# Cluster attention with two MLPs: similarities of heads 0 and 1 by float32 products, centroid words split later

## The chip, the core and the metric

The program runs on one core of one Trainium2 chip. The time is device microseconds (us) from start to end of one execution. Five engines work beside each other, each through its own list of instructions in order: TensorE (PE, products), VectorE (DVE), ScalarE (ACT), GpSimd (POOL) and SyncE (SP, which issues transfers). They wait for each other by semaphores.

## What is computed

```python
q_n, k_n, c_n = (x / (norm(x) + 1e-6) for x in (q, k, centroids))
q_assign = argmax(einsum('bhsd,hcd->bhsc', q_n, c_n))      # 16 clusters per head
k_assign = argmax(einsum('bhsd,hcd->bhsc', k_n, c_n))
mask = q_assign[:, :, :, None] == k_assign[:, :, None, :]
scores = where(mask, q @ k.T / 8, -1e9)
attn = exp(scores - max(scores)); attn /= sum(attn) + 1e-9
x = attn @ v                                               # 2 x 8 heads, 768 x 64
x = gelu-like MLP (512 -> 2048 -> 512), then gated MLP (512 -> 1536 -> 512)
```

q, k, v are 2 x 8 x 768 x 64, the centroids 8 x 16 x 64; all is float32.

## The kernel before

The 16 heads run one after the other; the two MLPs follow, planned by a list scheduler that the change leaves alone. All of the change lies in the first part, before and in the first two heads, whose order on each engine is the order in which the code is written.

A head's q and k come as one tile `stage` (q in partitions 0 to 63, k in 64 to 127, 768 columns). TensorE multiplies in float32r, so each of q and k is split in a high word (a cast, by `hi_q`, `hi_k` or single copies) and a low word (what is left, a subtraction by `lo_q`, `lo_k`). The tiles `q2`, `k2` hold these words in part 0; part 1 holds the high words and, in rows 64 to 79, the one-hot rows of the clusters. `extra_rows` clears part 1 of a head's tiles by three memsets on GpSimd.

The assignment of a head goes through these steps. `similar` multiplies the words of q and k by the centroids' words `cs`: four products of 128 x 384 into one PSUM tile `sims`. `largest` transposes that on VectorE (`T`, in 32 x 32 blocks), adds the two parts that belong to high and low words of the centroids (L603), and takes the maximum and a weighting; `assign` finishes the one-hot and transposes it back (`oT`, two halves). The q rows of the one-hot are then written by ScalarE (L637), the k rows by GpSimd (L638, two casts of 16 x 384). After that `smax` multiplies part 1 of q2 by part 1 of k2 and VectorE reduces the result to row maxima (`nm`); `mrow` and `st` follow, and the exponentials `p` on ScalarE.

For `cs` the centroids are normalised on VectorE (`cn`, L538), transposed by TensorE into the PSUM tile `ctp` (L543), split into `ch` and `cl` on VectorE (L552, L553) and spread by three ScalarE copies (L557, L559). `keep_warm(n)` is n products of zeros that nobody reads. `load_qk(h)` are two transfers by SyncE, which wait until `stage` is free. Four `stage` tiles and five slots of `q2`, `k2` go round.

The one-hot of head 0 is made in a stretch of its own; that of head 1 beside the scores of head 0, and `smax` of head 1 is TensorE's next work after the last scores of head 0.

Of the kernel before, what the change touches and what calls it, by code (L numbers as in the profile page):

```python
# [8 lines left out]
F32 = mybir.dt.float32  # L9
# [3 lines left out]
ACTF = mybir.ActivationFunctionType  # L13
ALU = mybir.AluOpType
# [170 lines left out]
def tile_cluster_attention_two_mlps(ctx: ExitStack, tc: tile.TileContext, qk, v, cen, w1, w2, wg, wv, w3, out):  # L185
# [233 lines left out]
    def q2(h):  # L419
        return q2_t[h % NQK]  # L420

    def k2(h):
        return k2_t[h % NQK]

    def load_qk(h):
        b, hh = divmod(h, H)
        for i in range(2):
            nc.sync.dma_start(out=stage[h % NST][i * D:(i + 1) * D], in_=qk[b, hh, :, i, :])
# [9 lines left out]
    def hi_q(h, copy=nc.scalar.copy):  # L438
        src = stage[h % NST][0:D].unsqueeze(1)
        copy(q2(h)[0:D], src.to_broadcast([D, 2, S]))  # L440

    def hi_k(h):
        src = stage[h % NST][D:2 * D]
        nc.scalar.copy(k2(h)[D:2 * D, 0, :], src)
        nc.scalar.copy(k2(h)[0:D, 1, :], src)

    def lo_q(h, eng=nc.vector):
        t = q2(h)
        eng.tensor_tensor(
            out=t[D:2 * D, 0, :], in0=stage[h % NST][0:D], in1=t[0:D, 0, :].bitcast(F32), op=ALU.subtract  # L450
        )

    def lo_k(h, eng=nc.vector):
        t = k2(h)
        eng.tensor_tensor(
            out=t[0:D, 0, :], in0=stage[h % NST][D:2 * D], in1=t[D:2 * D, 0, :].bitcast(F32), op=ALU.subtract
        )
# [32 lines left out]
    def keep_warm(n):  # L490

        ps = ps_o.tile([128, 512], F32, tag="o", name="warm")
        for _ in range(n):
            nc.tensor.matmul(out=ps, lhsT=zeros[:, 0:128], rhs=zeros)  # L494
# [7 lines left out]


    LEAD = 128 - 2 * NC
    nc.gpsimd.memset(cs.bitcast(F32), 0.0)

    def extra_rows(i):
        for t in (q2_t[i], k2_t[i]):
            nc.gpsimd.memset(t[D:MROW, 1, :].bitcast(F32), 0.0)
        nc.gpsimd.memset(k2_t[i][MROW:MROW + 1, 1, :].bitcast(F32), 1.0)  # L510
# [3 lines left out]
    for i in range(NC):  # L514
        nc.vector.memset(wd[:, :, i:i + 1], float(NC - i))
    nc.gpsimd.memset(v_t[0][:, :, D:D + 1], 1.0)
    for i in range(1, 3):
        extra_rows(i)
    s1 = acst.tile([128, 1], F32, name="s1")
    s2 = acst.tile([128, 1], F32, name="s2")  # L520
    for i in range(4):
        nc.gpsimd.memset(s1[32 * i:32 * i + 32], 1.0 if i % 2 else BIG)
        nc.gpsimd.memset(s2[32 * i:32 * i + 32], -1.0 if i % 2 else 0.0)


    sq = am_p.tile([128, HALF], F32, tag="U", name="U")[:, 0:D]
    nc.vector.tensor_tensor(out=sq, in0=craw, in1=craw, op=ALU.mult)
# [13 lines left out]
    ctp = ps_x.tile([128, 128], F32, tag="x", name="ctp")  # L541
    keep_warm(7)
    nc.tensor.transpose(out=ctp, in_=cn.rearrange("p a d -> p (a d)"), identity=ident)  # L543
    keep_warm(5)


    ks, qs = stage[0][D:2 * D], stage[0][0:D]
    nc.scalar.copy(q2(0)[0:D, 0, :], qs)
    nc.scalar.copy(k2(0)[D:2 * D, 0, :], ks)
    ch = acst.tile([128, 128], F32R, name="ch")  # L550
    cl = acst.tile([128, 128], F32R, name="cl")
    nc.vector.tensor_copy(ch, ctp)  # L552
    nc.vector.tensor_tensor(out=cl, in0=ctp, in1=ch.bitcast(F32), op=ALU.subtract)  # L553
    lo_q(0)
    to = cs[:, :, LEAD:].rearrange("p i (h x) -> p i h x", x=128)
    of = [t.rearrange("p (h c) -> p h c", c=NC) for t in (ch, cl)]
    nc.scalar.copy(to[:, :, :, 0:NC], of[0].unsqueeze(1).to_broadcast([128, 2, H, NC]))  # L557
    for i, r in enumerate((slice(0, D), slice(D, 2 * D))):
        nc.scalar.copy(to[r, i, :, NC:2 * NC], of[1][r])  # L559
    lo_k(0)  # L560
    nc.scalar.copy(k2(0)[0:D, 1, :], ks)
    nc.scalar.copy(q2(0)[0:D, 1, :], qs)
    ident_r = acst.tile([128, 128], F32R, name="ident_r")

    def similar(hs, pl=ps_x, tag="x"):


        out = []
        for h in hs:
            ps = take_bank(pl, tag, [128, 512], "sims")[:, 0:HALF]  # L570
            todo = [(i, n) for i in (0, 1) for n in range(2)]
            for at, (i, n) in enumerate(todo):
                o = LEAD + 128 * (h % H) - 32 * (2 * n + i)
                nc.tensor.matmul(  # L574
                    out=ps,
                    lhsT=cs[:, i, o:o + 128],
                    rhs=(q2, k2)[i](h)[:, 0, n * HALF:(n + 1) * HALF],
                    start=(at == 0),
                    stop=(at == len(todo) - 1),
                )  # L580
            out.append(ps)
        return out
# [9 lines left out]
    def largest(hs, pss):  # L592


        T = T_t[hs[0]] = am_p.tile([128, HALF], F32, tag="T", name="T")
        for j, ps in enumerate(pss):
            U = T if len(hs) == 1 else am_p.tile([128, HALF], F32, tag="U", name="U")
            nc.vector.transpose(out=U, in_=ps)
            yield
            of = U.rearrange("p (g a c) -> p g a c", a=2, c=NC)  # L600
            to = T.rearrange("p (g a c) -> p g a c", a=2, c=NC)[:, :, j, :]
            if len(hs) == 1:
                nc.vector.tensor_tensor(out=to, in0=of[:, :, 0, :], in1=of[:, :, 1, :], op=ALU.add)  # L603
            else:
                nc.vector.tensor_reduce(out=to.unsqueeze(3), in_=of.rearrange("p g a c -> p g c a"), axis=AX.X, op=ALU.add)
            yield
        Tv = groups(hs, T)
        G = Tv.shape[1]
        mx = sm_p.tile([128, HALF // NC, 1], F32, tag="mx", name="mx")[:, 0:G]
        nc.vector.tensor_reduce(out=mx, in_=Tv, axis=AX.X, op=ALU.max)  # L610
        yield
        nc.vector.tensor_tensor(out=Tv, in0=Tv, in1=mx.to_broadcast([128, G, NC]), op=ALU.is_equal)
        yield
        nc.vector.tensor_tensor(out=Tv, in0=Tv, in1=wd.to_broadcast([128, G, NC]), op=ALU.mult)  # L614
        yield
# [3 lines left out]
    def assign(hs, copies=(nc.scalar.copy, nc.scalar.copy)):  # L619

        T = T_next[0] = T_t.pop(hs[0])
        Tv = groups(hs, T)
        G = Tv.shape[1]
        mx2 = sm_p.tile([128, HALF // NC, 1], F32, tag="mx", name="mx2")[:, 0:G]
        nc.vector.tensor_reduce(out=mx2, in_=Tv, axis=AX.X, op=ALU.max)
        yield
        nc.vector.tensor_tensor(out=Tv, in0=Tv, in1=mx2.to_broadcast([128, G, NC]), op=ALU.is_equal)
        yield
        if len(hs) == 2:
            nc.vector.tensor_scalar(out=Tv, in0=Tv, scalar1=s1, scalar2=s2, op0=ALU.mult, op1=ALU.add)  # L630
        yield
        oT = am_p.tile([64, 2, HALF], F32, tag="oT", name="oT")
        for n in range(2):
            nc.vector.transpose(out=oT[:, n, :], in_=T[64 * n:64 * n + 64, :])  # L634
            if len(hs) == 1:
                rows = slice(ONE, ONE + NC), 1, slice(n * HALF, (n + 1) * HALF)
                nc.scalar.activation(q2(hs[0])[rows], oT[0:NC, n, :], ACTF.Copy, scale=BIG, bias=-BIG)  # L637
                nc.gpsimd.tensor_copy(k2(hs[0])[rows], oT[32:32 + NC, n, :])  # L638
            yield
        for j, h in enumerate(hs if len(hs) == 2 else ()):  # L640
            for i, dst in enumerate((q2(h), k2(h))):
                to = dst[ONE:ONE + NC, 1, :]
                o = 32 * i + NC * j
                rows = oT[o:o + NC].rearrange("p n s -> p (n s)")
                if j == 0:
                    copies[i](to, rows)
                else:
                    nc.sync.dma_start(out=to.bitcast(F32), in_=rows)

    def do(steps):  # L650
        for _ in steps:
            pass
# [213 lines left out]
    takes = {}  # L866
    for h in range(5, 5 + EARLY_ITEMS, 2):
        takes.update({(h, 2): (0,), (h, 3): (1,), (h, 4): (0,), (h, 5): (2,), (h + 1, 3): (1, 2)})
    sims = similar([0])
    keep_warm(18)  # L870
    hi_k(1)
    dummy = sm_p.tile([128, 1], F32, tag="dummy", name="dummy")
    nc.scalar.activation(dummy, y0, ACTF.Exp)
    do(largest([0], sims))

    do(assign([0]))
    hi_q(1)
    nc.vector.tensor_copy(ident_r, ident)
    lo_k(1, nc.gpsimd)
    lo_q(1, nc.gpsimd)  # L880
    hi_k(2)
    lo_k(2, nc.gpsimd)
    extra_rows(3)
    load_qk(4)
    load_qk(5)
    maxima = [(c, n) for m in range(2) for c in range(3 * m, 3 * m + 3) for n in range(2)]
    for i in range(SC):
        smax(0, *maxima[i], *((ps_m, "m"), (ps_m, "m"), (ps_s, "s"), (ps_s, "s"), (ps_s, "s"))[i % 5])
# [9 lines left out]
    for c in range(SC):  # L898
        scores(0, c, 0)
        if c < 2:  # L900
            smax(0, *maxima[10 + c], ps_m, "m")
        if c == 1:
            mneg(0, slice(SC // 2, SC))
            sims = similar([1])
            do(largest([1], sims))
        if c == 3:
            mrow_at_once(0, 1, ps_o, "o")
    for c in range(SC):
# [801 lines left out]
```

## Time and profile before

| | us |
|---|---|
| median of 3 runs | 769.22 (769.13 to 771.26) |
| the profiled execution | 769.23 |
| its span, first to last instruction | 767.4 |
| PE busy in the span | 759.5 |
| DVE busy | 667.4 |
| ACT busy | 492.9 |
| POOL busy | 148.6 |

The span is shorter than the time by 1.83 us, which lie before the first and behind the last instruction. TensorE is the engine that is nearly always busy; a change at the program's head is worth what it moves the start of TensorE's unbroken work.

### The profile page before, as it was taken

How to read it: one execution, taken by the hardware profiler on the slowest of the kernel's cores; microseconds unless marked ns; L12 is line 12 of the kernel's file. 1: busy time of each engine (PE TensorE's matmuls, PEld its weight loads, DVE VectorE, ACT ScalarE, POOL GpSimd, SP SyncE). 2: the span in 40 equal slices, each digit the busy share in tenths (PEclk: the TensorE clock that was granted, in tenths of full speed). 3: DMA queues.
4: the chain of work that ended last, by engine and by line, in shares of the span. 5: the costliest groups of instructions: out<-in, count | busy, mean ns of one | idle time of the engine just before them, and what ended most of it. 6: DMA issues, size and time to landing. Idle time of an engine off the chain costs nothing.

```text
span 767.4 us, 11983 instructions
## 1 busy us (share of the span) xinstructions
PE 759.5 (99%) x4194; PEld 659.5 (86%) x4194; DVE 667.4 (87%) x1224; ACT 492.9 (64%) x861; POOL 148.6 (19%) x165
## 2 busy tenths in 40 slices
PE   8999999999999999999999999999999999999998
PEld 6996676767677999999999999999999999999996
DVE  7899899999966999999797889999987997877752
ACT  7867798886686887677676776676453644443322
POOL 8847465746452000000000000000000000000000
PEclk9999999999999999999999999999999999999999
DMA  4132365843215787633277763667232122312102
GB/s 122 45 103 70 94 164 126 212 100 71 75 42 186 259 257 228 196 132 111 95 259 243 266 221 124 222 215 241 94 124 94 56 83 96 128 53 83 56 0 83
DMA packets 53388, 104.11 MB, mean 136 GB/s; under 512 B 19776, under 2 KB 25264, under 8 KB 53328
## 3 DMA queue, kind: packets, MB, share of 16 engines
q1 hardware_dynamic: 53104, 103.02, 43.1%
q8 instruction: 33, 0.54, 0.3%
q10 hardware_dynamic: 224, 0.33, 0.2%
q14 instruction: 27, 0.22, 0.1%
HBM read 76.23 MB, written 21.06 MB: 127 GB/s over the span
## 4 chain that ended last, share of the span: by engine, by line
PE 88%; DVE 10%; issue 1%; ACT 1%; DVEq 0%; ACTq 0%
PE h L384 37%; PE a L384 29%; PE st L711 7%; PE pv L749 6%; PE smax L661 4%; DVE nm L666 3%; PE ps L749 2%; PE pv L820 1%; PE sims L574 1%; DVE b L379 1%; PE warm L494 0%; DVE wo L291 0%; DVE T L614 0%; DVE s L1253 0%; DVE oT L634 0%
## 5 line engine op out<-in xcount | busy, mean ns | idle before, releaser
L384 PE MATMUL h<-xc,b 128*128 128x384 f32 x1680 | 316.6, 337 | 0.1
L384 PEld LDWEIGHTS h<-xc,b 128*128 128x128 f32 x1680 | 291.6, 188 | 10.0 <-DVE u L1309 2.3
L384 PE MATMUL a<-g,sp 128*128 128x512 f32 (+1 forms) x768 | 144.3, 336 | 0.0
L384 PEld LDWEIGHTS a<-g,sp 128*128 128x128 f32 x768 | 124.9, 188 | 16.9
L384 PE MATMUL a<-sp,g 128*128 128x512 f32 x432 | 109.6, 393 | 0.0
L721 ACT ACTIVATE p<-st 128x384 f32<-128x384 f32 x192 | 88.0, 491 | 28.4 <-PE st L711 23.4
L666 DVE TENSOR_REDUCE nm<-smax 128x1 f32<-128x384 f32 x192 | 97.1, 554 | 5.9 <-PE smax L661 5.4
L711 PE MATMUL st<-q,k 128*128 128x384 f32 (+1 forms) x384 | 98.3, 346 | 0.1
L384 PEld LDWEIGHTS a<-sp,g 128*128 128x128 f32 x432 | 80.1, 188 | 13.2
L376 ACT CAST b<-s 128x512 fp32r<-128x512 f32 x80 | 49.5, 620 | 55.5 <-PE h L384 45.7
L711 PEld LDWEIGHTS st<-q,k 128*128 128x128 f32 (+1 forms) x384 | 68.2, 190 | 10.4 <-issue 7.8
L737 POOL TENSOR_TENSOR add<-add,p 128x384 f32<-128x384 f32 x78 | 76.2, 1007 | 0.0
L661 PE MATMUL smax<-k,q 80*128 80x384 f32 x192 | 63.6, 347 | 1.4 <-DVE nm L666 0.6
L1309 DVE TENSOR_TENSOR u<-h,p 128x384 f32<-128x384 f32 x80 | 44.3, 554 | 22.8 <-PE h L384 22.6
L749 PE MATMUL pv<-p,v 128*64 128x384 f32 x336 | 60.2, 494 | 0.0
L280 ACT ACTIVATE a<-raw 128x512 f32<-128x512 f32 x68 | 45.7, 672 | 19.0 <-issue 9.4
L379 DVE TENSOR_TENSOR b<-s,b 128x512 fp32r<-128x512 f32 x80 | 54.8, 687 | 1.9 <-ACT b L376 0.7
L379 DVE TENSOR_TENSOR g<-c,g 128x768 fp32r<-128x768 f32 x56 | 53.5, 969 | 1.5 <-ACT g L376 0.9
L376 ACT CAST g<-c 128x768 fp32r<-128x768 f32 x56 | 45.3, 835 | 12.4 <-DVE c L1324 11.8
L286 DVE SCALAR_TENSOR_TENSOR t<-a,t 128x512 int32<-128x512 int32 x68 | 46.1, 684 | 3.4 <-ACT t L283 3.4
L1317 ACT ACTIVATE c<-c 128x384 f32<-128x384 f32 (+1 forms) x56 | 38.3, 685 | 16.5 <-DVE c L1309 15.8
L376 ACT CAST b<-w 128x768 fp32r<-128x768 f32 x35 | 29.2, 835 | 29.7 <-PE h L384 29.6
(146 smaller groups left out, 913.5 us busy)
## 6 DMA issues: line engine op xcount, KB each, us to landing
raw<-in_w SPq DMA_DIRECT2D x44, 512.0 KB
w<-scr SPq DMA_DIRECT2D x30, 512.0 KB
raw<-in_wg SPq DMA_DIRECT2D x12, 512.0 KB
raw<-in_wv SPq DMA_DIRECT2D x12, 512.0 KB
w<-scrg SPq DMA_DIRECT2D x12, 512.0 KB
w<-scrv SPq DMA_DIRECT2D x12, 512.0 KB
st<-in_qk SPq DMA_DIRECT2D x31, 192.0 KB
scr<-wd SPq DMA_DIRECT2D x23, 256.0 KB
```

Of the source, the lines that this page charges most:

```text
L280: nc.scalar.activation(a, raw[:, :, 1].bitcast(F32), ACTF.Copy, scale=2.0**-112)
L286: nc.vector.scalar_tensor_tensor(out=t, in0=a.bitcast(I32), scalar=3, in1=t, op0=ALU.logical_shift_left, op1=ALU.bitwise_or)
L376: nc.scalar.copy(to, of)
L379: eng.tensor_tensor(out=to, in0=of, in1=hi.bitcast(F32), op=ALU.subtract)
L384: nc.tensor.matmul(out=out_ps, lhsT=lhs[a], rhs=rhs[b], start=(start and j == 0), stop=(stop and j == 2), skip_group_check=True, **kw)
L661: nc.tensor.matmul(out=ps, lhsT=q2(h)[0:ONE + NC, 1, c * 128:(c + 1) * 128], rhs=k2(h)[0:ONE + NC, 1, n * HALF:(n + 1) * HALF],)
L666: nc.vector.tensor_reduce(out=nm_t[h][:, c, n:n + 1], in_=ps, axis=AX.X, op=ALU.max)
L711: nc.tensor.matmul(out=ps, lhsT=k2(h)[0:rows, a, c * 128:(c + 1) * 128], rhs=q2(h)[0:rows, a, at], start=(a == 0), stop=(a == 1),)
L721: nc.scalar.activation(p_t[h, c][:, n * HALF:(n + 1) * HALF], ps, ACTF.Exp, scale=scale)
L737: nc.gpsimd.tensor_tensor(out=add_t[h][:, at], in0=before[:, at], in1=p_t[h, c][:, at], op=ALU.add)
L749: nc.tensor.matmul(out=ps[n * D:(n + 1) * D, 0:HALF], lhsT=w, rhs=x[:, n * HALF:(n + 1) * HALF], start=start, stop=stop, skip_group_check= ...
L1309: lambda: nc.vector.tensor_tensor(out=to.tile[:, part], in0=ps.tile[:, 0:HALF], in1=other.tile, op=ALU.add),
```

## The change

Heads 0 and 1 get their similarities from `similar_first`: two float32 products (no split into words) of the whole `stage` tile, one for each half of the 768 columns, with the weights `first_w`, 128 x 64 for a head: the centroids stand in columns 0 to 15 for the q partitions and in columns 32 to 47 for the k partitions, zeros elsewhere. The halves land in partitions 0 to 63 and 64 to 127 of the same PSUM tile. `first_w` is cleared on GpSimd and filled by two small VectorE copies from `ctp`. In `largest` the addition for one head falls away.

Around it, work is moved. The high word of q of head 0 is cast on VectorE, its k low word is made on GpSimd after the one-hot's casts, `ch` is cast on ScalarE from `ctp` and `cl` subtracted on GpSimd; the three copies into `cs` stand behind `hi_q(1)`. The identity's cast goes to ScalarE. One `keep_warm` has 2 products in place of 5. The activation that brings the table of exponentials stands ahead of ScalarE's casts. Of head 2, the second copy of k's high word becomes a transfer (`bits`), and `extra_rows(2)` and the memsets of `s1`, `s2` stand behind `lo_k(2)` on GpSimd. `load_qk(5)` is issued after the similarities of head 1.

```diff
     nc.gpsimd.memset(v_t[0][:, :, D:D + 1], 1.0)
-    for i in range(1, 3):
-        extra_rows(i)
+    extra_rows(1)
...
-    keep_warm(5)
+    keep_warm(2)
+    nc.scalar.activation(dummy, y0, ACTF.Exp)
     ks, qs = stage[0][D:2 * D], stage[0][0:D]
-    nc.scalar.copy(q2(0)[0:D, 0, :], qs)
+    nc.vector.tensor_copy(q2(0)[0:D, 0, :], qs)
+    for i, rows in enumerate((slice(0, D), slice(D, 2 * D))):
+        nc.vector.tensor_copy(
+            first_w[rows, :, 2 * NC * i:2 * NC * i + NC], ctp[rows, 0:2 * NC].rearrange("p (h c) -> p h c", c=NC)
+        )
+    def similar_first(h, pl, tag):
+        ps = take_bank(pl, tag, [128, 512], "sims")[:, 0:HALF]
+        for n in range(2):
+            nc.tensor.matmul(
+                out=ps[n * D:(n + 1) * D], lhsT=first_w[:, h], rhs=stage[h][:, n * HALF:(n + 1) * HALF],
+                start=True, stop=True, skip_group_check=True,
+            )
+        return [ps]
+    sims = similar_first(0, ps_s, "s")
+    keep_warm(18)
+    lo_q(0)
...
-    nc.vector.tensor_copy(ch, ctp)
-    nc.vector.tensor_tensor(out=cl, in0=ctp, in1=ch.bitcast(F32), op=ALU.subtract)
+    nc.scalar.copy(ctf, ctp)
+    nc.scalar.copy(ch, ctp)
+    nc.scalar.copy(ident_r, ident)
+    nc.gpsimd.tensor_tensor(out=cl, in0=ctf, in1=ch.bitcast(F32), op=ALU.subtract)
...
-            if len(hs) == 1:
-                nc.vector.tensor_tensor(out=to, in0=of[:, :, 0, :], in1=of[:, :, 1, :], op=ALU.add)
...
     do(assign([0]))
+    lo_k(0, nc.gpsimd)
     hi_q(1)
-    nc.vector.tensor_copy(ident_r, ident)
     lo_k(1, nc.gpsimd)
     lo_q(1, nc.gpsimd)
-    hi_k(2)
+    centroid_words()
+    nc.scalar.copy(k2(2)[D:2 * D, 0, :], stage[2][D:2 * D])
+    bits(k2(2)[0:D, 1, :], k2(2)[D:2 * D, 0, :])
     lo_k(2, nc.gpsimd)
+    extra_rows(2)
     extra_rows(3)
+    for i in range(4):
+        nc.gpsimd.memset(s1[32 * i:32 * i + 32], 1.0 if i % 2 else BIG)
+        nc.gpsimd.memset(s2[32 * i:32 * i + 32], -1.0 if i % 2 else 0.0)
     load_qk(4)
-    load_qk(5)
...
-            sims = similar([1])
-            do(largest([1], sims))
+            do(largest([1], similar_first(1, ps_x, "x")))
+            load_qk(5)
```

VectorE, from the centroids' normalised tile `cn` to the one-hot of head 0 (`q_0` and `k_0` are the word tiles of head 0, `st` a `stage` tile), before:

```order
L538 TENSOR_SCALAR cn<-craw,y_262 128x128
L552 CAST ch<-ctp 128x128
L553 TENSOR_TENSOR cl<-ctp,ch 128x128
L449 TENSOR_TENSOR q_0_165<-st_194,q_0_165 64x768
L455 TENSOR_TENSOR k_0_166<-st_194,k_0_166 64x768
L598 STREAM_TRANSPOSE T<-sims 128x384
L603 TENSOR_TENSOR T<-T 128x12x16
L610 TENSOR_REDUCE mx<-T 128x12
```

The same place now:

```order
L535 TENSOR_SCALAR cn<-craw,y_253 128x128
L546 CAST q_0_165<-st_194 64x768
L548 COPY first_w<-ctp 64x2x16 x2
L449 TENSOR_TENSOR q_0_165<-st_194,q_0_165 64x768
L618 STREAM_TRANSPOSE T<-sims 128x384
L628 TENSOR_REDUCE mx<-T 128x12
```

The split of the centroids and the low word of k have left VectorE's list, a cast and two copies have come, and the addition is gone.

GpSimd, from the one-hot casts of head 0 (`k_0<-oT`) to those of head 1 (`k_1<-oT`), before:

```order
L638 CAST k_0_166<-oT 16x384 x2
L455 TENSOR_TENSOR k_1_189<-st_195,k_1_189 64x768
L449 TENSOR_TENSOR q_1_188<-st_195,q_1_188 64x768
L455 TENSOR_TENSOR k_2_181<-st_196,k_2_181 64x768
L509 MEMSET q_3_175 32x768
L509 MEMSET k_3_176 32x768
L510 MEMSET k_3_176 1x768
L638 CAST k_1_189<-oT 16x384 x2
```

The same place now (eight memsets of 32 x 1 stand between the last two rows):

```order
L656 CAST k_0_166<-oT 16x384 x2
L455 TENSOR_TENSOR k_0_166<-st_194,k_0_166 64x768
L455 TENSOR_TENSOR k_1_189<-st_195,k_1_189 64x768
L449 TENSOR_TENSOR q_1_188<-st_195,q_1_188 64x768
L455 TENSOR_TENSOR k_2_181<-st_196,k_2_181 64x768
L511 MEMSET q_2_180 32x768
L511 MEMSET k_2_181 32x768
L512 MEMSET k_2_181 1x768
L511 MEMSET q_3_175 32x768
L511 MEMSET k_3_176 32x768
L512 MEMSET k_3_176 1x768
...
L656 CAST k_1_189<-oT 16x384 x2
```

A subtraction, three large memsets and eight small ones have come between the two pairs of casts.

## Rows read from the trace of the kernel before

**Rows 1.** The page: busy time of engines, and POOL in 40 slices.
```profile
PE 759.5 (99%) x4194; PEld 659.5 (86%) x4194; DVE 667.4 (87%) x1224; ACT 492.9 (64%) x861; POOL 148.6 (19%) x165
...
POOL 8847465746452000000000000000000000000000
```

**Rows 2.** Chain that ended last, in time: start us, us, what, up to `smax`.
```profile
4.91 0.46 PE ctp L543
...
7.02 0.96 DVE k L455
...
8.12 0.60 PE sims L574 x2
...
8.75 0.59 DVE T L598
...
9.37 0.37 DVE T L603
...
11.71 0.58 DVE oT L634
...
13.05 0.43 PE smax L661
```

**Rows 3.** Timeline of PE, several windows: start us, us, engine, line, instructions, idle before.
```profile
1.52 3.36 PE L494 MATMUL warm<-q 128*128 128x512 f32 x7 [1.52 <-DVE y L498]
...
6.01 0.88 PE L494 MATMUL warm<-q 128*128 128x512 f32 x3
...
25.83 0.74 PE L661 MATMUL smax<-k,q 80*128 80x384 f32 x3
...
59.95 1.51 PE L749 MATMUL pv<-p,v 128*64 128x384 f32 x8
...
61.79 2.80 PE L749 MATMUL pv<-p,v 128*64 128x384 f32 x16
```

**Rows 4.** Timeline of DVE, the head of the program and two later places.
```profile
4.35 0.41 DVE L538 TENSOR_SCALAR cn<-craw,y 128x128 f32<-128x128 f32 x1
5.39 0.29 DVE L552 CAST ch<-ctp 128x128 fp32r<-128x128 f32 x1 [0.63 <-PE ctp L543]
...
24.40 0.95 DVE L440 CAST q<-st 64x1536 fp32r<-64x1536 f32 x1
...
36.31 2.07 DVE L614 TENSOR_TENSOR T<-T,wd 128x384 f32<-128x384 f32 x1
...
41.41 0.55 DVE L646 CAST q<-oT 16x768 fp32r<-16x768 f32 x1
```

**Rows 5.** Timeline of ACT up to the one-hot rows of head 0.
```profile
3.27 0.20 ACT L531 ACTIVATE y<-ss 128x1 f32<-128x1 f32 x1 [0.46 <-DVE ss L530]
...
8.45 0.83 ACT L444 CAST k<-st 64x768 fp32r<-64x768 f32 x1
...
10.15 1.28 ACT L873 ACT_TABLE_LOAD   x1
...
12.38 1.07 ACT L637 ACTIVATE q<-oT 16x384 fp32r<-16x384 f32 x2 [0.73 <-DVE oT L634]
```

**Rows 6.** Timeline of POOL, memsets, one-hot casts and subtractions.
```profile
5.68 0.73 POOL L509 MEMSET q<- 32x768 f32 x1
...
10.11 0.09 POOL L522 MEMSET s<- 32x1 f32 x1
...
12.35 1.16 POOL L638 CAST k<-oT 16x384 fp32r<-16x384 f32 x2 [1.61 <-DVE oT L634]
13.59 1.83 POOL L455 TENSOR_TENSOR k<-st,k 64x768 fp32r<-64x768 f32 x1
...
19.25 0.73 POOL L509 MEMSET q<- 32x768 f32 x1
...
24.43 1.29 POOL L638 CAST k<-oT 16x384 fp32r<-16x384 f32 x1
...
35.94 2.04 POOL L449 TENSOR_TENSOR q<-st,q 64x768 fp32r<-64x768 f32 x1
```

More of the change, by code (lines that the diff above doesn't have):

```diff
@@ L504, in tile_cluster_attention_two_mlps @@
     LEAD = 128 - 2 * NC
+    first_w = acst.tile([128, 2, D], F32, name="first_w")
+    nc.gpsimd.memset(first_w, 0.0)
     nc.gpsimd.memset(cs.bitcast(F32), 0.0)
@@ L516, in tile_cluster_attention_two_mlps @@
     nc.gpsimd.memset(v_t[0][:, :, D:D + 1], 1.0)
-    for i in range(1, 3):
-        extra_rows(i)
+    extra_rows(1)
     s1 = acst.tile([128, 1], F32, name="s1")
     s2 = acst.tile([128, 1], F32, name="s2")
-    for i in range(4):
-        nc.gpsimd.memset(s1[32 * i:32 * i + 32], 1.0 if i % 2 else BIG)
-        nc.gpsimd.memset(s2[32 * i:32 * i + 32], -1.0 if i % 2 else 0.0)
     sq = am_p.tile([128, HALF], F32, tag="U", name="U")[:, 0:D]
@@ L543, in tile_cluster_attention_two_mlps @@
     nc.tensor.transpose(out=ctp, in_=cn.rearrange("p a d -> p (a d)"), identity=ident)
-    keep_warm(5)
+    keep_warm(2)
+    dummy = sm_p.tile([128, 1], F32, tag="dummy", name="dummy")
+    nc.scalar.activation(dummy, y0, ACTF.Exp)
     ks, qs = stage[0][D:2 * D], stage[0][0:D]
-    nc.scalar.copy(q2(0)[0:D, 0, :], qs)
+    nc.vector.tensor_copy(q2(0)[0:D, 0, :], qs)
[3 more added lines that the diff above has]
+        )
@@ L549, in tile_cluster_attention_two_mlps @@
+    def similar_first(h, pl, tag):
[9 more added lines that the diff above has]
+    lo_q(0)
     nc.scalar.copy(k2(0)[D:2 * D, 0, :], ks)
+    nc.scalar.copy(k2(0)[0:D, 1, :], ks)
@@ L550, in tile_cluster_attention_two_mlps @@
+    nc.scalar.copy(q2(0)[0:D, 1, :], qs)
+    ctf = acst.tile([128, 128], F32, name="ctf")
     ch = acst.tile([128, 128], F32R, name="ch")
     cl = acst.tile([128, 128], F32R, name="cl")
-    nc.vector.tensor_copy(ch, ctp)
-    nc.vector.tensor_tensor(out=cl, in0=ctp, in1=ch.bitcast(F32), op=ALU.subtract)
[L554 to L562, printed above, removed]
-    ident_r = acst.tile([128, 128], F32R, name="ident_r")
+    nc.scalar.copy(ctf, ctp)
+    nc.scalar.copy(ch, ctp)
+    ident_r = acst.tile([128, 128], F32R, name="ident_r")
+    nc.scalar.copy(ident_r, ident)
+    nc.gpsimd.tensor_tensor(out=cl, in0=ctf, in1=ch.bitcast(F32), op=ALU.subtract)
@@ L565, in similar, with centroid_words @@
+    def centroid_words():
+        to = cs[:, :, LEAD:].rearrange("p i (h x) -> p i h x", x=128)
+        of = [t.rearrange("p (h c) -> p h c", c=NC) for t in (ch, cl)]
+        nc.scalar.copy(to[:, :, :, 0:NC], of[0].unsqueeze(1).to_broadcast([128, 2, H, NC]))
+        for i, r in enumerate((slice(0, D), slice(D, 2 * D))):
+            nc.scalar.copy(to[r, i, :, NC:2 * NC], of[1][r])
     def similar(hs, pl=ps_x, tag="x"):
@@ L599, in largest @@
             yield
-            of = U.rearrange("p (g a c) -> p g a c", a=2, c=NC)
-            to = T.rearrange("p (g a c) -> p g a c", a=2, c=NC)[:, :, j, :]
-            if len(hs) == 1:
-                nc.vector.tensor_tensor(out=to, in0=of[:, :, 0, :], in1=of[:, :, 1, :], op=ALU.add)
-            else:
+            if len(hs) == 2:
+                of = U.rearrange("p (g a c) -> p g a c", a=2, c=NC)
+                to = T.rearrange("p (g a c) -> p g a c", a=2, c=NC)[:, :, j, :]
                 nc.vector.tensor_reduce(out=to.unsqueeze(3), in_=of.rearrange("p g a c -> p g c a"), axis=AX.X, op=ALU.add)
@@ L868, in tile_cluster_attention_two_mlps @@
         takes.update({(h, 2): (0,), (h, 3): (1,), (h, 4): (0,), (h, 5): (2,), (h + 1, 3): (1, 2)})
-    sims = similar([0])
-    keep_warm(18)
     hi_k(1)
-    dummy = sm_p.tile([128, 1], F32, tag="dummy", name="dummy")
-    nc.scalar.activation(dummy, y0, ACTF.Exp)
     do(largest([0], sims))
     do(assign([0]))
+    lo_k(0, nc.gpsimd)
     hi_q(1)
-    nc.vector.tensor_copy(ident_r, ident)
     lo_k(1, nc.gpsimd)
     lo_q(1, nc.gpsimd)
-    hi_k(2)
+    centroid_words()
+    nc.scalar.copy(k2(2)[D:2 * D, 0, :], stage[2][D:2 * D])
+    bits(k2(2)[0:D, 1, :], k2(2)[D:2 * D, 0, :])
     lo_k(2, nc.gpsimd)
+    extra_rows(2)
     extra_rows(3)
+    for i in range(4):
+        nc.gpsimd.memset(s1[32 * i:32 * i + 32], 1.0 if i % 2 else BIG)
+        nc.gpsimd.memset(s2[32 * i:32 * i + 32], -1.0 if i % 2 else 0.0)
     load_qk(4)
-    load_qk(5)
     maxima = [(c, n) for m in range(2) for c in range(3 * m, 3 * m + 3) for n in range(2)]
```

## Prediction, made before the changed kernel ran

> **What bounds the kernel now.** I read the page first: TensorE is busy for 759.5 of 767.4 us [rows 1], so 7.9 us is all that it waits, and an edit at the head of the program pays only if TensorE's unbroken work begins earlier. GpSimd's slices show where a second engine counts: it is busy in the first third and idle behind it. The chain of waits, in order of time, then says what the head consists of [rows 2]: the transposed centroids at 4.91, the splits on VectorE up to the low word of k (7.02 to 7.98), the last two similarity products at 8.12, VectorE's one-hot from 8.75 to the transposes at 11.71, the first maxima's product at 13.05. Last I read the timelines of single engines [rows 3 to 6], to see who is next when this chain gets shorter. The next place is the first products `smax` of head 1: the second of them starts at 25.83 [rows 3], 0.11 us after GpSimd's second one-hot cast of head 1 ends (24.43 + 1.29 = 25.72, [rows 6]). In the kernel before, GpSimd and TensorE arrive there together.
>
> **Step 1, the similarities of head 0.** VectorE is done with `cn` at 4.76 [rows 4]. The new cast of q is 768 columns wide; the row of that width took 0.55 [rows 4], so it runs from 4.79 to 5.34, behind the transpose, whose result VectorE took up at 5.39 [rows 4]. The two copies into `first_w` read 32 columns each from PSUM; the row with 128 columns took 0.29, so each lies between nothing and 0.29; I take 0.2, nearer to that row since its fixed part is in it. They end at 5.82, and with the 0.14 from VectorE to TensorE that rows 2 show (7.98 to 8.12) the products could start at 5.96. TensorE has two zero products to do first; the third of the old five started at 6.01 [rows 3], so that is the start. Their price is that of `pv`, which has the same shape (64 weights wide, 384 columns, float32, both halves): eight records in 1.51 and sixteen in 2.80, that is 0.16 a record and 0.22 behind the last [rows 3]. Two products are four records, so 0.87, and they end at 6.88. This is at the full clock of 2.4 GHz: the seven zero products from 1.52 took 0.48 each, near 512 columns at 1.2 GHz (0.43), the three from 6.01 took 0.29 each with their tail, near 2.4 GHz, and TensorE had worked without a break from 1.52 on. If the two products fall at the lower level they take 1.73 by the same rows. VectorE's transpose starts at 6.92 in place of 8.75: 1.83 earlier. `lo_q(0)` ends by 6.8 and hides under the products. The addition falls away (0.37 and its gap, 0.39, [rows 2]). Together **2.22 earlier** at the one-hot transposes.
>
> **Step 2, a collision on the way.** `cl` is now subtracted on GpSimd when `ch` is there, at about 8.2, while VectorE is in `is_equal` and the weighting, two operations with two inputs in SBUF. Rows show such a pair excluding each other: VectorE's weighting at 36.31 took 2.07, to 38.38, against GpSimd's subtraction from 35.94 to 37.98 [rows 4, 6], though half the width costs 0.37 [rows 2]. A subtraction of 768 columns takes 1.83 [rows 6], so one of 128 lies between 0.3 and 0.5. I charge 0.25; bounds 0 and 0.5. That leaves **1.97**. ScalarE is no gate: from 3.47, a table load of 1.28, 0.2 for its activation, five casts at 0.85 and three small ones at 0.3 end at 10.14, and the one-hot's first half comes at 12.38 less 1.97 = 10.41 [rows 5]. The 18 zero products, too, end before `smax`, at about 11.
>
> **Step 3, GpSimd between two heads.** Its casts for head 0 start at 12.35 less 1.97 = 10.38. Then, before those of head 1: the two casts with their gap 1.24 (12.35 to 13.59); four subtractions, one more than before, at 1.89 (three of them from 13.59 to 19.25); two `extra_rows`, one more than before, at 2.21 (two of them from 5.68 to 10.11); eight memsets of 0.09, at most 0.7 [rows 6]. Sum 1.24 + 7.55 + 4.43 + 0.7 = 13.92, so head 1's casts can start at 24.30. The one-hot of head 1 is there much earlier, its addition being gone as well: GpSimd is the gate. Undisturbed the casts take 1.16 and end at 25.46.
>
> **Step 4, what delays GpSimd more.** In the old trace its second cast took 1.29 in place of 0.58, since VectorE's cast of head 2's q ran from 24.40 to 25.35 [rows 4, 6]: while that cast holds, GpSimd stands, a loss of 0.71. Now VectorE reaches that cast at about 22, when GpSimd is in its memsets. No row has such a memset against such a cast: the cost is between nothing and 0.95, the cast's length. The nearest row, the cast on GpSimd, gives 0.71, and I take that, since a memset writes SBUF as the cast did. The casts of head 1 then start at 25.01 and end at 26.17, and the second `smax` starts at 26.28, against 25.83: **0.45 later than before**.
>
> The Trainium skill's page "SBUF — State Buffer", section "Who interferes with whom", says that a VectorE cast in its two-port mode and a GpSimd operation exclude each other for a whole instruction, and that only operations with two SBUF inputs spare a GpSimd operation that merely writes. By that rule the memsets stand behind the cast and the sum is 769.7; if merely writing spared them here too, it would be 769.0. The trace agrees for a cast on GpSimd (1.29 against 0.58); for a memset no run here shows it.
>
> **What follows.** TensorE's list has `smax` of head 1 next, so it waits for GpSimd whatever it gained: its own arrival would be 25.83 less 1.97 = 23.86. Behind that place TensorE, VectorE and GpSimd go on with the same lists as before, and the shift goes through to the end. GpSimd and VectorE keep their distance to about 0.1, so the collision at 36.31 stays. Costed at nothing: the `cs` copies (ScalarE has from 12.9 to 15, before the row of maxima is due), the transfer that replaces a copy of head 2 (needed some 25 us later; behind it on SyncE wait only loads of head 4 and later, used after 25), `load_qk(5)`, which had to wait for GpSimd's low words of head 1 anyhow, and the two float32 products of head 1 (0.65 by the records, four products of 0.16 before).
>
> The profiled execution took 769.23, the median is 769.22, so the sum stands against both: 769.23 + 0.45 = **769.7**.
>
> **Rivals.**
> - *Memsets are not held up by a cast.* Then GpSimd ends at 25.46, the second `smax` starts at 25.57: 0.26 gained, **769.0**. For it: no memset row is visibly stretched. Against it: the stretched cast. Without the collision of step 2 it is 768.7.
> - *GpSimd is no gate*, because its rows are rough and the memsets overlap more than I add. Then TensorE's own 1.97 come through: **767.3**. Against it: 1.7 to 2.4 us would have to vanish from a sum of 13.9.
> - *The similarity products fall at the lower clock*, or VectorE's first cast has to stand behind a memset (0.6 late, a like price): 0.87 more through the chain to GpSimd, **770.6**. Against it: the clock rose at about 6.0 while TensorE worked without a break, as it does now.
> - *Slower: TensorE loses its clock while it waits for GpSimd.* It would wait from 23.86 to 26.28, 2.4 us, and rows show no such hole. If the granted clock then falls to 1.2 GHz and comes back as slowly as at the start (at the lower level from 1.52 to about 6.0, [rows 3]), 4.5 us of work take twice their time: 2.25 more, **771.9**. It decides from the wait's length on: the 0.63 to 1.61 us for which engines wait in these rows are shorter, and none of them is TensorE's.
> - *The change doesn't do what it says*, the two float32 halves running one by one at some higher price than `pv`: that goes with the 770.6.
>
> The skill's "TensorE: Matmul & The Clock Gate", section "What's actually happening", says that the throttled clock is the default and activity releases it, which bears on the slower rival; whether this wait is long enough no run here shows.
>
> **How the numbers follow.** Chances: forecast 0.44; memsets not held up 0.32; GpSimd no gate 0.05; lower clock or a late cast 0.08; TensorE's clock lost 0.08; the rest, delays further on that I don't see, 0.03. About 0.3% (2.3 us, so below 766.9 or above 771.5) can be told from no change by a measurement of this kernel. The range reaches from 768.4 (the second case without the collision and with copies that cost nothing) to 770.9 (the lower clock, with the cast's full 0.95): it holds the first two and the fourth case, 0.84. Faster by over 0.3% takes the third case and more, 0.03; slower is the clock's loss and part of the rest, 0.09; within is 0.88.
>
> **What would show it.** The two float32 products near 6.0 and together about 0.9 long; the transposes of head 0's one-hot at 9.5 to 9.8; GpSimd's casts of head 1 at 25.0 (24.3 in the rival), with no idle time before them; a memset of about 1.5 us beside VectorE's cast at 22; TensorE waiting about 2 us ahead of `smax` of head 1. The forecast is wrong if GpSimd idles there, or if the time moves by over 1 us behind 26 us.

## The result and the profile after

The changed kernel takes 775.58 us (median of 22 runs, 768.85 to 777.45), the kernel before 769.64 (22 runs, 768.90 to 771.26): a ratio of 1.0056, with a 95% interval of 1.0039 to 1.0073. It is slower, by 5.9 us; the forecast was 769.7, a tie.

The runs of the changed kernel fall in two groups, told apart by TensorE's mean granted clock, and these groups are the finding. In 15 runs the clock was 0.988 to 0.991 and the time 775.47 to 777.45 (median 776.35); in 7 runs it was 0.999 or 1.000 and the time 768.85 to 770.47 (median 769.59, level with before). No run of the kernel before is below 0.999 (55 runs beside the experiments). The profiled execution is of the first group: 777.21, with a span of 775.4.

The page of the changed kernel: busy times, which answer to [rows 1], and the granted clock in 40 slices.

```profile
PE 767.2 (99%) x4191; PEld 665.6 (86%) x4191; DVE 664.5 (86%) x1221; ACT 491.4 (63%) x862; POOL 151.2 (19%) x168
...
PEclk9689999999999999999999999999999999999999
```

TensorE is busy 7.7 us longer with three instructions fewer, and the second and third slices (19 to 58 us) show a 6 and an 8 where the clock was granted in part. Both are seen closer in TensorE's timeline (start, us, engine, line, instructions, idle time before and who ended it):

```profile
6.11 0.87 PE L556 MATMUL sims<-st,first_w 128*64 128x384 f32 x4
...
22.73 1.31 PE L729 MATMUL st<-q,k 128*128 128x384 f32 x6
25.21 1.46 PE L679 MATMUL smax<-k,q 80*128 80x384 f32 x4 [1.17 <-POOL k L656]
26.47 2.65 PE L838 MATMUL pv<-v,p 128*128 128x65 f32 x12
...
39.91 2.12 PE L729 MATMUL st<-q,k 128*128 128x384 f32 x6
41.83 2.07 PE L838 MATMUL pv<-v,p 128*128 128x65 f32 x12
43.70 1.30 PE L729 MATMUL st<-q,k 128*128 128x384 f32 x6
44.84 1.45 PE L838 MATMUL pv<-v,p 128*128 128x65 f32 x12
...
49.83 0.95 PE L679 MATMUL smax<-k,q 80*128 80x384 f32 x4
```

The similarities stand at 6.11 and last 0.87. At 24.04 TensorE has reached `smax` of head 1 and waits 1.17 for GpSimd. Behind that, twelve `pv` products take 2.65 (26.47) where the same twelve take 1.45 at 44.84; six `st` products take 2.12 (39.91) and then 1.30 (43.70). Stretches of this trace (window, its us, PE busy and instructions, granted clock, DMA share, GB/s) say why:

```profile
25.50:26.00 0.50, 0.49 (x3) 1.00 0.00 0
26.00:26.50 0.50, 0.50 (x4) 0.55 0.00 0
...
42.50:43.00 0.50, 0.50 (x4) 0.50 0.00 0
43.00:44.00 1.00, 1.00 (x9) 0.94 0.00 0
```

1.00 is 2.4 GHz and 0.50 is 1.2 GHz, and a stretch with a value in between holds some time at each. 0.55 from 26.00 to 26.50 is 0.05 us at the upper level and 0.45 at the lower: the clock falls at about 26.05, 0.8 us behind the end of the wait. 0.94 from 43.00 to 44.00 puts its rise at about 43.12. In between, for 17.1 us, TensorE works at the lower level without a pause. `smax` of head 2 starts at 49.83; the kernel before has it at 42.67, 7.16 earlier. The rows of the kernel before at this place, with the first `smax` of head 1 and the `pv` behind it:

```profile
25.65 0.92 PE L661 MATMUL smax<-k,q 80*128 80x384 f32 x4
26.41 1.45 PE L820 MATMUL pv<-v,p 128*128 128x65 f32 x12
...
42.67 0.93 PE L661 MATMUL smax<-k,q 80*128 80x384 f32 x4 [0.43 <-DVE k L646]
```

GpSimd's and VectorE's timelines show what TensorE waited for, first GpSimd:

```profile
10.28 1.04 POOL L656 CAST k<-oT 16x384 fp32r<-16x384 f32 x2 [1.20 <-DVE oT L652]
...
22.52 0.73 POOL L512 MEMSET k<- 1x768 f32 x1
23.29 0.81 POOL L902 MEMSET s<- 32x1 f32 x1
...
24.51 0.09 POOL L903 MEMSET s<- 32x1 f32 x1
24.66 0.95 POOL L656 CAST k<-oT 16x384 fp32r<-16x384 f32 x2
```

```profile
7.01 0.58 DVE L618 STREAM_TRANSPOSE T<-sims 128x384 f32<-128x384 f32 x1
...
9.58 1.18 DVE L652 STREAM_TRANSPOSE oT<-T 64x384 f32<-64x384 f32 x2
...
22.46 1.60 DVE L440 CAST q<-st 64x1536 fp32r<-64x1536 f32 x1
```

A memset of 32 x 1 takes 0.81 beside VectorE's cast of head 2's q, against 0.09 for the others; the cast itself, 0.95 in the kernel before [rows 4], takes 1.60. The memset of 22.52 runs at its usual 0.73 to 23.25, so it is the cast that stood behind it first, and the next two memsets behind the cast.

### The profile page after: what moved, and what is told of

Same layout as the page of the kernel before. It is cut to its first block, busy times and chain, and to the rows that moved or that the text cites. A ratio compares the mean times of both kernels' runs of the same rounds, so it can differ in the third digit from the quotient of the medians.

```text
span 775.4 us, 11982 instructions
## 1 busy us (share of the span) xinstructions
PE 767.2 (99%) x4191; PEld 665.6 (86%) x4191; DVE 664.5 (86%) x1221; ACT 491.4 (63%) x862; POOL 151.2 (19%) x168
## 4 chain that ended last, share of the span: by engine, by line
PE 87%; DVE 7%; POOL 1%; DMA 1%; ACT 1%; issue 1%; SPq 0%; POOLq 0%; ACTq 0%; DVEq 0%
PE h L384 38%; PE a L384 30%; PE st L729 6%; PE pv L767 5%; DVE nm L684 3%; PE smax L679 3%; PE pv L838 2%; PE ps L767 2%; PE sims L594 1%; DMA st<-in_qk 1%; POOL k L455 0%; DVE oT L652 0%; DVE st L472 0%; DVE wo L291 0%; DVE t L286 0%
## 5 line engine op out<-in xcount | busy, mean ns | idle before, releaser
L679 PE MATMUL smax<-k,q 80*128 80x384 f32 x192 | 65.3, 357 | 1.9 <-POOL k L656 1.2
```

Of the source, the lines that this page charges most:

```text
L679: nc.tensor.matmul(out=ps, lhsT=q2(h)[0:ONE + NC, 1, c * 128:(c + 1) * 128], rhs=k2(h)[0:ONE + NC, 1, n * HALF:(n + 1) * HALF],)
```

## The experiments

The theory (A): the change makes TensorE wait ahead of `smax` of head 1, this wait costs the granted clock, and without the wait the change is worth nothing either way. The rival (B): the lower clock comes from the other work, above all the float32 products and the order of the head.

### The wait filled

Behind the last `pv(0, 0)`, ahead of `smax` of head 1, six products of zeros that nobody reads:

```diff
+    for _ in range(2):
+        ps = take_bank(ps_m, "m", [128, 512], "fill")
+        for _ in range(3):
+            nc.tensor.matmul(out=ps, lhsT=zeros[:, 0:128], rhs=zeros)
     lo_q(2, nc.gpsimd)
```

> The changed kernel with six products of zeros (128 x 512) in TensorE's list ahead of the first smax of head 1, in the place where it waited 1.17 us for GpSimd. Theory A (the wait costs the clock): TensorE stays busy through the place, the granted clock reads 1.000 in every run and the time is that of the changed kernel's runs at full clock, 769.3 (768.8 to 770.3). Theory B (the clock falls because of the work ahead of the place: float32 products 64 wide, fewer products of zeros, and the wait is only where it shows): the clock still falls in about two runs of three and the median stays near 776.

Measured: 770.41 (11 runs, 769.45 to 770.77), ratio 1.0006 (0.9998 to 1.0015), and a clock of 0.999 or 1.000 in all 11. TensorE's timeline:

```profile
23.87 1.54 PE L937 MATMUL fill<-q 128*128 128x512 f32 x6
25.34 1.25 PE L679 MATMUL smax<-k,q 80*128 80x384 f32 x4
26.43 0.78 PE L838 MATMUL pv<-v,p 128*128 128x65 f32 x6
```

Useless work takes 5.2 us off the changed kernel's median. GpSimd is still the gate of `smax`, and `pv` behind it starts at 26.43; in the kernel before at 26.41. So A holds for the loss, and what the change won up to 23.87 is given back at this place.

### Half of the wait filled

The same with two products in place of six.

> The changed kernel with two products of zeros (128 x 512, 0.26 us each, read by nobody) in place of the six of the run that filled the wait: TensorE works 0.5 us of the 1.2 us that it would wait ahead of smax of head 1, and waits about 0.65. Theory A (the wait costs the clock; any wait that is left can cost it): some runs fall as with the 0.68 us wait of the variant without the memsets, and take 775 to 782; the rest take 769.3 to 770.4. Rival (a wait below about 0.7 us that follows dense products leaves the clock alone): all runs at full clock, 769.3 to 770.4.

Measured: 770.69 (10 runs, 769.12 to 776.22), ratio 1.0021 (0.9998 to 1.0043). In 3 of 10 runs the clock fell (774.99, 776.00, 776.22; clock 0.991 to 0.993). The profiled execution is one of the three; TensorE's timeline and two stretches:

```profile
24.54 0.63 PE L937 MATMUL fill<-q 128*128 128x512 f32 x2
26.01 1.24 PE L679 MATMUL smax<-k,q 80*128 80x384 f32 x4 [0.84 <-POOL k L656]
```

```profile
28.00:30.00 2.00, 2.00 (x13) 0.71 0.16 35
...
38.00:40.00 2.00, 2.00 (x10) 0.73 0.00 0
```

The clock falls at about 28.8 and is back at 39.1, after 10.2 us. With the profile's wait of 0.84 the clock is lost now and then; with 1.17 it was lost in 15 of 22.

### The wait alone, in the kernel before

The kernel before, with five memsets on GpSimd (of a row that already holds ones) ahead of head 1's casts:

```diff
+    for _ in range(HOLE):                                   # HOLE = 5
+        nc.gpsimd.memset(k2_t[3][MROW:MROW + 1, 1, :].bitcast(F32), 1.0)
     load_qk(4)
```

> The kernel before, with five more memsets of 768 columns on GpSimd (a row that already holds ones) ahead of its one-hot casts of head 1, so that TensorE waits about 1.2 us ahead of smax of head 1, at about 25.6 to 26.8; nothing else is changed. Theory A: the granted clock falls behind the wait in many runs, and those take 6 to 8 us more, about 776; runs at full clock take 770 to 770.8. Theory B: the clock stays at 1.000 and the time is 770.2 to 770.9.

Measured: 771.12 (12 runs, 770.59 to 778.69), ratio 1.0042 (1.0022 to 1.0063). The clock fell in 4 of 12 runs (775.64, 776.13, 776.55, 778.69), in none of the kernel before beside it. The profiled execution, 771.0, kept its clock:

```profile
26.72 1.24 PE L662 MATMUL smax<-k,q 80*128 80x384 f32 x4 [0.91 <-POOL k L639]
```

Nothing of the change is in this kernel, so B falls as far as it needs the change: a wait made by GpSimd alone is enough. Seven memsets in place of five:

> The kernel before with seven memsets in place of five, so that TensorE waits some 2.3 us in place of 0.9 ahead of smax of head 1. Theory A with the wait's length as the dose: the clock falls in most of the runs (over 8 of 12), median 777 to 780; runs at full clock 772.3. If the length does not matter, a third of the runs again and a median of 772.3.

Measured: 779.48 (4 runs, 778.41 to 779.78), ratio 1.0117 (1.0104 to 1.0131); all 4 fell, with clocks of 0.989 to 0.991. Its trace:

```profile
28.30 1.25 PE L662 MATMUL smax<-k,q 80*128 80x384 f32 x4 [2.48 <-POOL k L639]
```

```profile
29.50:30.00 0.50, 0.50 (x6) 0.69 0.00 0
...
42.00:44.00 2.00, 2.00 (x10) 0.67 0.00 0
```

The second fence is of stretches: the clock falls at about 29.7 and is back at about 43.3. The delay itself is 2.65 of the 9.6 us (779.48 less the 769.91 of the kernel before beside it) by `smax`, at 28.30 against 25.65; the rest came with the clock. And five memsets with the six products of zeros ahead of `smax`:

> The kernel before with the same five memsets on GpSimd as in the run named hole, and six products of zeros on TensorE in the place of the wait. Theory A: the clock falls in none of the runs (it fell in 4 of 12 without the products), time 770.6 to 771.6, as the runs of hole at full clock. If the fall came from GpSimd's or VectorE's shift and not from TensorE's idle time, it comes in a third of the runs again.

Measured: 770.97 (11 runs, 770.26 to 772.09), ratio 1.0011 (1.0003 to 1.0020), clock 0.999 or 1.000 in all. The same delay, filled, costs 1.1 us (against 769.91) and no clock; a shift of GpSimd or VectorE without TensorE's idle time does not take it:

```profile
25.68 1.54 PE L921 MATMUL fill<-q 128*128 128x512 f32 x6
27.05 0.92 PE L662 MATMUL smax<-k,q 80*128 80x384 f32 x4
```

### Wide products behind the wait

Why does the clock stay low for 17.1 us in which TensorE is always busy? Here the changed kernel gets twelve products of 384 columns, read by nobody, behind the first four `smax` of head 1; the wait stays.

```diff
                 beside(1, c, ((ps_m, "m"), (ps_s, "s")))
+                for _ in range(2 if c == 0 else 0):
+                    ps = take_bank(ps_m, "m", [128, 512], "dense")[:, 0:HALF]
+                    for _ in range(6):
+                        nc.tensor.matmul(out=ps, lhsT=ident_r, rhs=k2(1)[:, 0, 0:HALF])
```

> The changed kernel with twelve more products of 384 columns that nobody reads, on TensorE behind the first four smax of head 1, in the stretch in which the clock stayed at its lower level from 26 to 43 us; its wait ahead of smax is left as it was. Theory: the clock stayed low because the stretch holds mostly products of 65 columns with a weight load each; with dense work in it the clock comes back by about 34, some 9 us sooner, and the falls are shorter. At full clock the products cost about 1.5 us; a run with a fall takes 774 to 776, against 776 to 778 if the dense work does not bring the clock back.

Measured: 772.84 (5 runs, 772.45 to 773.36), ratio 1.0034 (1.0022 to 1.0046), clocks of 0.997 to 1.000. TensorE's timeline and stretches of the profiled execution:

```profile
25.68 1.24 PE L679 MATMUL smax<-k,q 80*128 80x384 f32 x4 [1.32 <-POOL k L656]
26.77 3.91 PE L1128 MATMUL dense<-k,ident_r 128*128 128x384 f32 x12
```

```profile
26.00:27.00 1.00, 1.00 (x5) 1.00 0.00 0
27.00:28.00 1.00, 1.00 (x4) 0.50 0.00 0
...
30.00:31.00 1.00, 1.00 (x8) 0.79 0.75 221
```

The clock falls at 27.0 and is back at about 30.4, after 3.4 us in place of 17.1. The changed kernel with twelve useless products is 2.7 us faster than without. Three of the five runs fell (clock 0.997 or 0.998, 772.71 to 773.36) and two did not (1.000, 772.45 and 772.84): the products cost some 3 us with the clock kept, twice what was expected, and a fall then adds less than 1. By an estimate from the mean clocks, twice the missing share of the span, a fall here lasts 3 to 5 us and in the runs of the changed kernel 14 to 19. So what stands behind the fall sets its price. In the profile after TensorE first runs `pv` (65 columns) in turn with `smax`, and the clock stays low; before it rises stand four similarity products and six `st` products (39.91) of 384 columns, and the rise itself comes in the `pv` behind them. The other traces with a fall are alike: in `fill_half` it rises at 39.1 behind four similarity products, in `hole_long` among similarity and `st` products, and in no trace here while `pv` and `smax` took turns. Since `smax` has 384 columns too, width alone does not tell these stretches apart; what in the twelve products brought the clock back is not shown.

### The work that delays GpSimd put later

First all that the change put ahead of head 1's casts: `extra_rows(2)`, `extra_rows(3)` and the memsets of `s1`, `s2` stand behind `lo_q(3, nc.gpsimd)`.

> The changed kernel with GpSimd's memsets for heads 2 and 3 and for s1, s2 moved behind its subtractions of head 3, so that only four subtractions stand between the one-hot casts of heads 0 and 1. Theory A: GpSimd is free at 18.9, the casts of head 1 start at about 21.9 when VectorE's transposes are there, TensorE does not wait ahead of smax of head 1, the granted clock is 1.000 in every run; the 1.7 us that TensorE had gained by 24 us come through: 767.6 (767.0 to 768.5). Theory B: the clock falls as before, 775 to 776.

Measured: 778.16 (4 runs, 778.12 to 778.74), ratio 1.0112 (1.0097 to 1.0126), clock 0.986 or 0.987. The expectation failed. The wait at `smax` of head 1 is gone, but the memsets push GpSimd's subtractions for head 4 under VectorE's casts of head 2's one-hot, and TensorE waits there. Timelines of VectorE, GpSimd and TensorE:

```profile
39.39 1.15 DVE L664 CAST q<-oT 16x768 fp32r<-16x768 f32 x1
40.55 2.07 DVE L664 CAST k<-oT 16x768 fp32r<-16x768 f32 x1
```

```profile
38.28 1.83 POOL L455 TENSOR_TENSOR k<-st,k 64x768 fp32r<-64x768 f32 x1
40.19 2.01 POOL L449 TENSOR_TENSOR q<-st,q 64x768 fp32r<-64x768 f32 x1
```

```profile
24.73 0.90 PE L679 MATMUL smax<-k,q 80*128 80x384 f32 x4
...
42.72 0.95 PE L679 MATMUL smax<-k,q 80*128 80x384 f32 x4 [1.43 <-issue]
```

The trace names "issue", but the cast that `smax` reads ends at 42.62, 0.10 before `smax` starts. The clock falls at about 45.25 and is back at about 65.7: the same loss, at another wait. Then only the memsets of `s1`, `s2` put later:

> The changed kernel with only the eight small memsets of s1 and s2 moved behind the subtractions of head 3. They took 23.29 to 24.6 with the hold by VectorE's cast, which then falls on the casts themselves, so TensorE's wait of 1.17 us shrinks by about 0.6. Theory A: the clock falls in fewer runs than 15 of 22, or in none, median between 768.9 and 769.6 if it falls in less than half of them. Theory B: no difference, 776.

Measured: 781.02 (6 runs, 773.75 to 782.08), ratio 1.0123 (1.0091 to 1.0155); all fell. This expectation, too, failed: fewer falls were forecast, or no difference. The profiled execution (775.59) shows a wait of 0.68 ahead of `smax` of head 1, and the clock falls at about 27.6, behind it:

```profile
25.35 1.24 PE L679 MATMUL smax<-k,q 80*128 80x384 f32 x4 [0.68 <-POOL k L656]
```

That left the runs of 781 open, so the same kernel was profiled again:

> The variant with the memsets of s1 and s2 behind the low words of head 3, a second time, for a profile of a run of 780 to 782. Theory A: in such a run the clock falls twice, at smax of head 1 near 25 to 28 us and again at a later wait of TensorE in the first 80 us; or it falls once and stays for about 28 us in place of 14. Rival (the time comes from elsewhere): the granted clock comes back by 42 us and the 5 us stand at a place behind.

Measured: 780.89 (4 runs, 775.61 to 783.98), ratio 1.0136 (1.0093 to 1.0179). The profiled execution now is one of 780.72. TensorE, VectorE and GpSimd:

```profile
24.46 1.24 PE L679 MATMUL smax<-k,q 80*128 80x384 f32 x4 [0.42 <-POOL k L656]
...
43.98 1.62 PE L679 MATMUL smax<-k,q 80*128 80x384 f32 x4 [2.61 <-issue]
```

```profile
41.81 2.07 DVE L664 CAST k<-oT 16x768 fp32r<-16x768 f32 x1
```

```profile
41.60 1.85 POOL L455 TENSOR_TENSOR k<-st,k 64x768 fp32r<-64x768 f32 x1 [3.84 <-ACT k L444]
```

```profile
42.00:44.00 2.00, 0.02 (x1) 0.76 0.28 54
44.00:46.00 2.00, 2.00 (x8) 0.50 0.97 229
```

The clock survives the first wait (0.42); by the stretches of the last fence it falls inside the second, 2.61 long, at about 43.0. Neither of the two accounts expected was right: there is one fall, at another place. A run of this kernel either falls at the first wait, and then reaches head 2 so late that GpSimd's subtraction is long over (775.59: VectorE's cast of k takes 0.55, at 45.56), or it keeps its clock, arrives early, collides and falls there (780.72). Three of the ten runs lie at 773.75 to 775.61, seven at 780.72 to 783.98; two of the ten were profiled, one of each sort. That the other eight went one of these two ways is read from their times alone.

### Both places mended

`extra_rows(3)` goes behind head 4's subtractions, and these come forward, ahead of the time at which VectorE makes head 2's one-hot:

```diff
-    extra_rows(3)
...
+    hi_k(4)
+    hi_q(4)
+    lo_k(4, nc.gpsimd)
+    lo_q(4, nc.gpsimd)
+    extra_rows(3)
     extra_rows(4)
...
-    hi_k(4)
-    hi_q(4)
...
                 if i > 4:
                     hi_k(i)
                     hi_q(i)
-                lo_k(i, nc.gpsimd)
-                lo_q(i, nc.gpsimd)
+                    lo_k(i, nc.gpsimd)
+                    lo_q(i, nc.gpsimd)
```

> The changed kernel with the three memsets of head 3's tiles moved on GpSimd from ahead of head 1's one-hot casts to behind the subtractions of head 4, which come forward by that much, so that no subtraction slides under VectorE's casts at 39 to 42 us as in the run named late. Theory A (a wait of TensorE in this stretch costs the clock): GpSimd starts the casts of head 1 at 22.4 to 23.2 in place of 24.7, TensorE waits under 0.3 us ahead of smax of head 1, the granted clock is 1.000 in all or nearly all runs, and the 1.6 us that TensorE had gained by then come through less what the order behind it gives back: 767.7 (767.2 to 769). If instead the clock falls in most of the runs, theory A lacks a cause.

Measured: 767.89 (8 runs, 767.13 to 769.56), ratio 0.9974 (0.9964 to 0.9985), clock 0.999 or 1.000 in all: faster than both kernels. TensorE and VectorE:

```profile
25.77 0.90 PE L679 MATMUL smax<-k,q 80*128 80x384 f32 x4
...
42.14 0.96 PE L679 MATMUL smax<-k,q 80*128 80x384 f32 x4
```

```profile
36.29 0.56 DVE L632 TENSOR_TENSOR T<-T,wd 128x384 f32<-128x384 f32 x1
```

In this execution neither `smax` waits: GpSimd starts the casts of head 1 at 23.78, after 0.45 of idle time, so that VectorE and no longer GpSimd is the gate. The weighting that took 2.07 beside GpSimd [rows 4] takes 0.56. But this profile is of an execution (769.02) whose similarity products ran late and, by their length, at the lower rate (7.05, for 1.55), so that TensorE reached `smax` of head 1 only at 25.77. Whether it waits there in the faster runs no profile shows; the clock was kept in all 8. The change and these moves together are worth 2.0 us (against 769.91). Part of that is the moves' own: from the first `smax` of head 1 to that of head 2 it takes 16.37 here and 17.02 in the kernel before. What the moves would give there without the change was not run.

## Why the prediction was wrong

**Step 1 held.** The products start at 6.11 (forecast 6.01), take 0.87 (0.87), and the transpose starts at 7.01 (6.92).

**Step 2 held in the sum and not in the place.** If there was a collision it fell on GpSimd: `cl` took 0.61, estimated at 0.3 to 0.5, and VectorE's two operations took 0.36 each. The one-hot transposes start at 9.58 (9.74), GpSimd's casts at 10.28 (10.38). The terms for ScalarE add up to 10.10 and not 10.14; it is no gate either way.

**Steps 3 and 4 held in the mechanism, and were too dear.** GpSimd is the gate, without idle time before it, and the memsets are held by VectorE's cast: two rows of 0.81 and 0.79, side by side, in place of 0.09. The casts of head 1 start at 24.66 (forecast 25.01) and take 0.95 (1.16). The second `smax`, priced at 0.45 later than before (26.28), starts at 25.66 in the profile after, 0.17 earlier than before; by `pv` behind it, with the clock kept in `fill`, the difference is 0.02 later (26.43 against 26.41). The rule of the Trainium skill's page "SBUF — State Buffer", section "Who interferes with whom", which the forecast took, agrees with the rows: an operation of GpSimd that only writes stood behind the cast (0.81 in place of 0.09).

**What followed failed.** With the clock kept, the change does what was forecast, a tie: 769.59 in the 7 runs, 770.41 with the wait filled, against 769.7. The step that failed is "What follows": the sum let TensorE's wait for GpSimd cost the delay alone and the shift go through to the end, and left the granted clock to the rival "TensorE loses its clock while it waits for GpSimd", which was wrong in its chance and in its price. I gave it 0.08, since the rows showed no such wait of TensorE's (and I read them wrongly: the 1.52 ahead of its first product [rows 3] is one, at the program's start). That was no evidence against it: a state that the old trace does not contain has no row. TensorE arrived at 24.04 (forecast 23.86); the wait ahead of the first `smax` was 1.17 and not the 2.4 that I computed up to the second, and still the clock fell in 15 of 22 runs. For the price I took the recovery at the program's start, 4.5 us at the lower level, where TensorE runs products of 512 columns. It lasted 17.1 us behind this wait, where `pv` and `smax` come, and 3.4 in `dense`, with twelve products of 384 columns put ahead of them. My 2.25 became 6.8 (776.35 less 769.59).

**The rival of the similarities at the lower clock** was not what moved the time, yet it exists: in the kernel `late` the four records took 1.55 (row at 6.28 of its trace), in `tuned` 1.55, in `dense` 0.96, and 0.87 in the profile after. By these lengths, the time at which the clock rises at the start differs between executions.

**What stays open.** Which runs fall. Waits ahead of `smax` of head 1, as the profiles show them, and falls:

| kernel | wait, us | runs with a fall |
|---|---|---|
| filled (`fill`, `hole_fill`) | 0 | 0 of 22 |
| `fill_half` | 0.84 | 3 of 10 |
| before with five memsets (`hole`) | 0.91 | 4 of 12 |
| after | 1.17 | 15 of 22 |
| before with seven memsets (`hole_long`) | 2.48 | 4 of 4 |

The kernels with the longer waits fall more often. But each wait is that of one profiled execution, and the other runs of a kernel can wait longer or less: `somelate` fell behind 0.68 in one profile and not behind 0.42 in the other. Nor does the length alone decide, as `fill_half` fell behind 0.84 and `hole` kept its clock at 0.91. The kernel before, which waits 0.43 ahead of `smax` of head 2, kept it in all 55 runs. The Trainium skill's page "TensorE: Matmul & The Clock Gate", section "What's actually happening", says that the chip's look at the activity runs freely and is not set by the program's start. That would make it a matter of chance; no run here can show it.

## What to carry to other kernels

Work won ahead of a place where another engine is the gate turns into a wait of the bottleneck engine, and on TensorE the wait can cost more than its length: here 1.2 us of it cost 6.8. Price such a wait by the work that stands behind it (17.1 us at the lower level here, 3.4 with twelve wide products put ahead of it), and look for it at every later meeting of the two engines, not only the first. Move the gating engine's work, and run the new order several times; where that can't be done, fill the wait with products that nobody reads, as in `fill` (no fall in 11 runs).

## What the runs showed of the hardware

TensorE stayed at 1.2 GHz for 17.1 us without a pause in its work (26.05 to 43.12 in the profile after), for 10.2 in `fill_half` and 20.5 in `late`; with twelve products of 384 columns behind the fall it was back after 3.4. The fall mostly came when TensorE was at work again: 0.8 us after the wait's end in the profile after, 2.8 in `fill_half`, and within the wait only where it lasted 2.61 (the second profile of `somelate`). And one cast of VectorE, 16 x 768, took 2.07 in place of 0.55 beside a subtraction on GpSimd: a collision that appears or goes as the two engines' arrivals shift by some tenths of a microsecond.
